# A bonus row spread earlier, and loads held behind a weight transfer, in a fused RWKV and feed-forward kernel

## The chip, the cores and the metric

One Trainium2 chip, one of its cores. The metric is the time of the whole program on the device in microseconds (us), taken several times for each kernel. "Span" is the length of the profiled execution, some 1.7 us less than its time.

## The reference, cut to what matters

A recurrent attention over 768 steps, for 4 batches and 8 heads of 48 columns, then a feed-forward layer over the 3072 rows that come out:

```python
for t in range(S):
    kt, vt, rt = k[:, :, t], v[:, :, t], r[:, :, t]
    cur = np.einsum('bhd,bhe->bhde', u[None] * kt, vt)          # the bonus, row u
    y[:, :, t] = np.einsum('bhd,bhde->bhe', rt, state + cur)
    state = w[None, :, :, None] * state + np.einsum('bhd,bhe->bhde', kt, vt)
x = y.transpose(0, 2, 1, 3).reshape(B * S, H * D)               # 3072 x 384
h = x @ w_in                                                    # 384 x 2048
out = (h * sigmoid(h)) @ w_out                                  # 2048 x 384
```

## The kernel before

The kernel works in 24 units: 6 pieces of 128 steps for each of 4 batches. A unit has three loads, r, k and v, each 128 steps x 8 heads x 48 columns: 1024 packets of 192 bytes. They go to six sets of tiles. In r and k each head's 48 columns stand in 64, so a row of 192 bytes starts every 256 bytes; in v the rows follow each other without gaps.

```python
rin = [big.tile([128, H, 64], FP, name=f"rin{i}") for i in range(NIN)]   # 6 sets
kin = [big.tile([128, H, 64], FP, name=f"kin{i}") for i in range(NIN)]
vin = [big.tile([128, H, D], FP, name=f"vin{i}") for i in range(NIN)]
# ... cut ...
load_row(nc.sync, wrow, w)
load(0, (0,), nc.scalar)        # r of unit 0 on ScalarE's queue
load_row(nc.scalar, urow, u)    # the bonus row behind it
load(0, (1,))
load(1, (0, 1))
load(0, (2,))
load(1, (2,))
for i in range(2, B):
    load(i)
```

At the start TensorE turns the row w into columns, transposes r of unit 0, turns the bonus row u into columns, transposes k of unit 0, and spreads u over 128 partitions (u_bc). GpSimd needs u_bc for its first product.

```python
spin(6)                         # matmuls on zeros, to keep TensorE going
wT = to_cols(wrow, None)
spin(3)
# ... cut ...
p1(0, mid=[cols_u, rows_u])     # between the transposes of r and of k
p1(1)
nat_ku(0)                       # GpSimd: k * u_bc
nat_rk(0)                       # GpSimd: r * that; VectorE then sums it per head
```

Later both halves of the second layer's weights (768 KB each) go on GpSimd's queue, and at about the same time the loads of units 6 to 9 on SyncE's:

```python
gate = cst.tile([128, 1], FP)
# ... cut ...
wout_part(0)
# ... cut ...
wout_part(1)
# ... cut ...
for i in range(4):
    load(NIN + i)               # units 6 to 9
p2(b_, nxt=b_ + 1, late=True)
```

## Time and profile before

| kernel before | us |
|---|---|
| median of 3 runs | 199.02 (198.54 to 199.46) |
| span of the profiled run | 197.3 |
| TensorE busy | 189.2 |
| first product of GpSimd starts | 8.19 |
| k of unit 8 lands | 51.3 |

TensorE is all but full. What can be won lies in a few waits of TensorE, and which ones they are is read in the prediction below. First, the queues' shares: packets, megabytes, and the time that the packets took as a share of all 16 DMA engines. The load queue q1 of the kernel before:

```profile
q1 hardware_dynamic: 84940, 20.46, 48.1%
```

Second, the work of ScalarE from 7.6 us on (start, length, engine, line, operation):

```profile
7.99 0.51 ACT L178 CAST v<-vin 128x384 f16<-128x384 f32 x1
8.41 1.28 ACT L441 ACTIVATE lamCT<-pif 112x128 f32<-112x128 f32 x4
...
11.79 1.91 ACT L214 ACTIVATE vu<-vin,rku 128x48 f32<-128x48 f32 x8 [1.70 <-DVE rku L200]
```

The eight bonus multiplications start at 11.79 us.

### The profile page before, as it was taken

To read this page: it belongs to the slowest core of one execution; us is meant where nothing else is said; L and a number is where in the kernel's file an instruction comes from. 1 tells how busy PE (TensorE), PEld (TensorE's weight loads), DVE (VectorE), ACT (ScalarE), POOL (GpSimd) and SP (SyncE) were. 2 spreads that over 40 slices of the span, in tenths; PEclk is the share of its full clock that TensorE was granted. 3 is DMA by queue.
4 is the path that set the end of the run, shared out by engine and by line. 5 is a ranking of instruction groups with operands and counts; after the bars stand their busy time and mean duration, and the time that the engine had idled before them with its cause. 6 is when DMAs were issued, how large, how long until landed. Compare 5 with 4: busy or idle time off the path is not lost.

```text
span 197.3 us, 4925 instructions
## 1 busy us (share of the span) xinstructions
PE 189.2 (96%) x1918; PEld 127.4 (65%) x1918; DVE 115.7 (59%) x233; ACT 91.0 (46%) x207; POOL 115.2 (58%) x145
## 2 busy tenths in 40 slices
PE   7969999899899999999999999999999999999993
PEld 2737878787666877675566766557666546644563
DVE  5867658885758764975675686476576344210121
ACT  3464587799311626215961216682016680069300
POOL 4389969989966859697669647735437710000000
PEclk9999999999999999999999999999999999999999
DMA  5999997999788754665567377526371011210022
GB/s 115 220 168 139 145 230 152 174 182 195 152 192 211 163 114 104 146 138 129 119 120 139 103 176 163 104 59 121 94 190 43 20 22 43 79 60 0 3 81 80
DMA packets 89696, 24.12 MB, mean 122 GB/s; under 512 B 82888, under 2 KB 89672, under 8 KB 89672
## 3 DMA queue, kind: packets, MB, share of 16 engines
q1 hardware_dynamic: 84940, 20.46, 48.1%
q0 software_dynamic: 3680, 3.15, 10.7%
q10 hardware_dynamic: 1052, 0.20, 0.5%
q8 instruction: 15, 0.25, 0.5%
q14 instruction: 9, 0.07, 0.1%
HBM read 20.45 MB, written 4.72 MB: 128 GB/s over the span
## 4 chain that ended last, share of the span: by engine, by line
PE 72%; POOL 11%; DMA 9%; issue 3%; SPq 1%; DVE 0%; POOLq 0%
PE ops L373 30%; PE hps L361 24%; DMA kin<-in_k_dram 9%; PE ae L270 8%; PE xs L245 4%; POOL ku L183 3%; POOL rku_f L189 3%; POOL kc L194 2%; PE y L296 2%; POOL win L416 2%; PE y L293 2%; POOL vu L206 1%; PE ops L387 1%; PE sps L312 1%; SPq L69 1%
## 5 line engine op out<-in xcount | busy, mean ns | idle before, releaser
L364 ACT ACTIVATE gT<-hps 128x256 f16<-128x256 f32 (+1 forms) x128 | 59.8, 494 | 50.5 <-PE hps L361 48.9
L361 PE MATMUL hps<-xT,win 128*128 128x256 f16 (+1 forms) x384 | 69.2, 326 | 0.2
L373 PE MATMUL ops<-wout,gT 128*128 128x384 f16 x368 | 63.8, 326 | 0.0
L361 PEld LDWEIGHTS <-win 128*128 128x128 f16 x384 | 35.4, 98 | 22.9 <-issue 0.7
L373 PEld LDWEIGHTS <-gT 128*128 128x128 f16 x368 | 34.7, 98 | 22.4
L279 DVE TENSOR_TENSOR am<-ae,maskM 128x512 f16<-128x512 f32 x24 | 16.6, 691 | 31.9 <-PE ao L272 31.8
L377 DVE COPY osb<-ops 128x384 f32<-128x384 f32 x23 | 12.7, 554 | 28.9 <-PE ops L373 28.7
L183 POOL TENSOR_TENSOR ku<-kin,u_bc 128x384 f32<-128x384 f32 x24 | 24.2, 1006 | 7.0 <-ACT u_bc L152 5.4
L270 PEld LDWEIGHTS ae<-rk 48*128 48x128 f32 x192 | 23.1, 187 | 7.3 <-issue 4.7
L206 POOL TENSOR_TENSOR vu<-vin,rku 128x384 f32<-128x384 f32 x23 | 19.1, 832 | 14.6 <-DVE rku L200 14.5
L272 PE MATMUL ao<-rk 48*128 48x128 f32 x192 | 27.5, 284 | 0.0
L270 PE MATMUL ae<-rk 48*128 48x128 f32 x192 | 27.5, 284 | 0.0
L256 DVE TENSOR_TENSOR rk<-xs,pif 112x512 f32<-112x512 f32 x40 | 25.6, 681 | 1.7 <-PE xs L245 1.7
L262 ACT CAST rT<-rk 112x512 f16<-112x512 f32 x20 | 12.3, 616 | 29.7 <-DVE rk L256 29.7
L189 POOL TENSOR_TENSOR rku_f<-rin,ku 128x384 f32<-128x384 f32 x24 | 24.1, 1004 | 1.9
L194 POOL TENSOR_TENSOR kc<-kin,lamC 128x384 f16<-128x384 f32 x24 | 24.0, 1004 | 0.0
L272 PEld LDWEIGHTS ao<-rk 48*128 48x128 f32 x192 | 23.1, 187 | 0.0
L303 DVE TENSOR_TENSOR y<-y,vu 128x384 f16<-128x384 f32 x24 | 13.4, 557 | 8.3 <-POOL kc L194 2.5
L326 POOL CAST stb<-st 112x384 f16<-112x384 f32 x12 | 6.1, 504 | 20.7 <-DVE st L321 20.7
L279 DVE TENSOR_TENSOR am<-ao,maskM 128x512 f16<-128x512 f32 x24 | 16.3, 680 | 0.0
L200 DVE TENSOR_REDUCE rku<-rku_f 128x8 f32<-128x384 f32 x24 | 13.2, 550 | 3.2 <-POOL rku_f L189 2.7
L296 PE MATMUL y<-v,am 128*128 128x48 f16 x192 | 12.2, 185 | 2.8 <-ACT st L452 1.5
(73 smaller groups left out, 170.5 us busy)
## 6 DMA issues: line engine op xcount, KB each, us to landing
kin<-in_k_dram SPq DMA_DIRECT2D x24, 192.0 KB, 3.4
vin<-in_v_dram SPq DMA_DIRECT2D x24, 192.0 KB, 3.7
rin<-in_r_dram SPq DMA_DIRECT2D x23, 192.0 KB, 3.4
out_dram<-osb SPq DMA_DIRECT2D x23, 192.0 KB, 1.9
win<-in_moe_w_in_dram POOLq DMA_DIRECT2D x4, 384.0 KB, 5.7
wout<-in_moe_w_out_dram POOLq DMA_DIRECT2D x2, 768.0 KB, 11.5
xT<-y SPq DMA_TRANSPOSE x18, 2.3
rin<-in_r_dram ACTq DMA_DIRECT2D x1, 192.0 KB, 2.7
```

The source lines that it names most:

```text
L183: nc.gpsimd.tensor_tensor(out=L["ku"], in0=kin[i % NIN][:, :, 0:D], in1=u_bc, op=ALU.mult)
L189: nc.gpsimd.tensor_tensor(out=L["rku_f"], in0=rin[i % NIN][:, :, 0:D], in1=L["ku"], op=ALU.mult)
L194: nc.gpsimd.tensor_tensor(out=kc[i % NKC][:, :, 0:D], in0=kin[n][:, :, 0:D], in1=lamC, op=ALU.mult)
L206: nc.gpsimd.tensor_tensor(out=L["vu"], in0=vin[i % NIN], in1=L["rku"].unsqueeze(2).broadcast_to([128, H, D]), op=ALU.mult)
L256: nc.vector.tensor_tensor(out=rk[:, :, :, 64 * g:64 * g + 64], in0=xs[g][0:PR], in1=lam(g), op=ALU.mult)
L270: nc.tensor.matmul(ae[:, p, :], L["kT"][0:D, p, :], L["rT"][0:D, p, :], start=True, stop=True)
L272: nc.tensor.matmul(ao[:, p, :], L["kT"][64:PR, p, :], L["rT"][64:PR, p, :], start=True, stop=True)
L279: nc.vector.tensor_tensor(out=am, in0=a, in1=maskM.unsqueeze(1).broadcast_to([128, NP, C]), op=ALU.mult)
L296: nc.tensor.matmul(y[:, 2 * p + j, :], L["am"][j][:, p, :], v16[:, 2 * p + j, :], start=not sc, stop=(not sc or j == 1))
L361: nc.tensor.matmul(hps, win[:, q, ft * 128:(ft + 1) * 128], xts[sc][:, q, b0:b1, :].rearrange("p b t -> p (b t)"), start=(q == 0), stop=(q ...
L364: nc.scalar.activation(out=gts[sc][:, ft, b0 * C:b1 * C], in_=hps, func=AF.Silu)
L373: nc.tensor.matmul(ops, gts[sc][:, ft, b * C:(b + 1) * C], wout[:, ft, :], start=(ft == 0), stop=(ft == NFT - 1))
```

## The change

It has two parts. The start: the bonus row goes alone onto ScalarE's queue, r of unit 0 joins SyncE's, and u is spread ahead of unit 0. The hold: a copy of 128 bytes out of the first half of the second layer's weights stands in SyncE's queue ahead of unit 8, so that the loads behind it wait until that half is in. The diff, cut to its core:

```diff
 load_row(nc.sync, wrow, w)
-load(0, (0,), nc.scalar)
 load_row(nc.scalar, urow, u)
-load(0, (1,))
+load(0, (0, 1))
 # ... cut ...
 spin(6)
 wT = to_cols(wrow, None)
-spin(3)
+spin(2)
+ucol = to_cols(urow, nc.scalar.copy)
+spin(2)
 u_bc = cst.tile([128, H, D], FP)
 # ... cut ...
+to_rows(u_bc, lambda p: ucol[:, p:p + 1].broadcast_to([PR, 128]))
 # ... cut ...
 gate = cst.tile([128, 1], FP)
+held = cst.tile([1, 64], F16)
 # ... cut ...
-p1(0, mid=[cols_u, rows_u])
+p1(0)
 # ... cut ...
-for i in range(4):
-    load(NIN + i)
+load(NIN)
+load(NIN + 1)
+nc.sync.dma_start(out=held, in_=wout[0:1, 0, 0:64])
+load(NIN + 2)
+load(NIN + 3)
```

More of the change, by code (lines that the diff above doesn't have):

```diff
@@ L62, in unit, with load @@
         return divmod(i, B)
-    def load(i, which=(0, 1, 2), queue=nc.sync):
+    def load(i, which=(0, 1, 2)):
         if i >= NU:
@@ L68, in load @@
         for t, src in [((rin, r), (kin, k), (vin, v))[x] for x in which]:
-            queue.dma_start(out=t[i % NIN][:, :, 0:D],
+            nc.sync.dma_start(out=t[i % NIN][:, :, 0:D],
                               in_=src[b, :, sc * C:sc * C + C, :]
@@ L215, in bonus_act, with p1 @@
                                  func=AF.Copy, scale=L["rku"][:, h:h + 1])
-    def p1(i, spins=0, mid=()):
+    def p1(i, spins=0):
         n = i % NIN
@@ L226, in p1 @@
                 nc.tensor.transpose(t[0:PR, p, :], flat[:, 128 * p:128 * p + PR], ident)
-            if mid:
-                mid.pop(0)()
         rk = wrk.tile([PR, 2, NP, C], FP, name="rk")
@@ L422, in wout_part @@
             in_=moe_w_out[1024 * g:1024 * g + 1024, :].rearrange("(f p) n -> p f n", p=128))
-    def cols_u():
-        live["u"] = to_cols(urow, nc.scalar.copy)
-    def rows_u():
-        to_rows(u_bc, lambda p: live["u"][:, p:p + 1].broadcast_to([PR, 128]))
-    p1(0, mid=[cols_u, rows_u])
+    p1(0)
     p1(1)
```

## The prediction

> **What bounds the kernel now.** I read the page first (engine shares and the chain that ended last), then TensorE's waits, then the order of time on GpSimd, VectorE and TensorE in the first 20 us, and last the queue of SyncE with the DMA queues between 34 and 53 us.
>
> ```profile
> span 197.3 us, 4925 instructions
> PE 189.2 (96%) x1918; PEld 127.4 (65%) x1918; DVE 115.7 (59%) x233; ACT 91.0 (46%) x207; POOL 115.2 (58%) x145
> ```
>
> TensorE is busy for 189.2 of 197.3 us. 1.26 us pass before its first matmul and about 3 us after its last, so only some 4 us of idle time lie inside the program, and no change that leaves the arithmetic alone can win more than that. The waits of TensorE name it:
>
> ```profile
> PE y L296 <- ACT st L452: 1.5, 1, 1.5
> PE y L296 <- DVE am L279: 1.3, 4, 0.4
> PE spin L128 <- DVE wrow L80: 1.3, 1, 1.3
> PE xs L245 <- DMA kin<-in_k_dram: 0.5, 1, 0.5
> ```
>
> Two single waits matter, the first (at 13 to 14.5 us) and the last (at 50.7 to 51.3 us). After the second I find no further wait of TensorE up to its last matmul: from 51.7 us on whatever time TensorE has gained stays gained.
>
> The first wait is labelled with a ScalarE copy (L452) that ends at 14.48 us. I do not believe the label: the first weight load of that group waits on VectorE's semaphore, and the VectorE mask ends at 14.45 us. Its own history is this (start, length, engine, line, operation):
>
> ```profile
> 13.30 0.55 DVE L200 TENSOR_REDUCE rku<-rku_f 128x8 f32<-128x384 f32 x1 [1.54 <-POOL rku_f L189]
> 13.77 0.68 DVE L279 TENSOR_TENSOR am<-ae,maskM 128x512 f16<-128x512 f32 x1
> ```
> ```profile
> 8.19 1.01 POOL L183 TENSOR_TENSOR ku<-kin,u_bc 128x384 f32<-128x384 f32 x1 [5.45 <-ACT u_bc L152]
> 9.28 1.00 POOL L189 TENSOR_TENSOR rku_f<-rin,ku 128x384 f32<-128x384 f32 x1
> 10.22 0.93 POOL L416 DMA_DIRECT2D win<-in_moe_w_in_dram  x1
> 11.17 1.01 POOL L183 TENSOR_TENSOR ku<-kin,u_bc 128x384 f32<-128x384 f32 x1
> 12.27 1.00 POOL L189 TENSOR_TENSOR rku_f<-rin,ku 128x384 f32<-128x384 f32 x1
> ```
>
> GpSimd sits idle 5.45 us for u_bc, the bonus row spread over 128 partitions, then works without a break; VectorE's second reduction waits 1.54 us for GpSimd's second product; the mask of unit 1 stands behind that reduction, and TensorE behind the mask. So the arrival of u_bc at 8.1 us decides the first wait. The chain that ended last says the same: up to 34 us it runs on GpSimd.
>
> The second wait is for k of unit 8. SyncE's queue around it:
>
> ```profile
> 35.20 0.71 SPq L69 DMA_DIRECT2D rin<-in_r_dram  x1
> 36.02 0.71 SPq L69 DMA_DIRECT2D kin<-in_k_dram  x1
> 36.81 5.45 SPq L69 DMA_DIRECT2D vin<-in_v_dram  x1
> 42.36 4.85 SPq L69 DMA_DIRECT2D rin<-in_r_dram  x1
> 47.32 3.54 SPq L69 DMA_DIRECT2D kin<-in_k_dram  x1
> ```
>
> The k load is issued at 36.02 us and lands at 51.3 us, against a median of 3.4 us from issue to landing. In those 15 us both halves of the second layer's weights (issued by GpSimd at 34.96 and 38.45 us) are on the same engines. Counting packets by microsecond: from 43 to 48 us the weight queue moves about 190 packets of 768 bytes per us and the load queue about 190 of 192 bytes; alone the load queue moves some 1200. SyncE also stands still[...]. The first half of the weights lands at 45.5 us, the second at 50.8 us; their first use is at 48.0 us.
>
> **What the Trainium skill says.** "DMA: Bandwidth & Descriptors", section "Queues, rings and completion order": each DMA engine takes turns between the rings that have work, a packet at a time. The trace agrees with its 190 against 190 packets per us: a small packet pays one large packet's turn, which is why the loads crawl at about 36 KB per us. The same page, section "Issuing engines are not separate DMA queues": starting transfers from several engines saves only sequencer time. Here that is half true: r of unit 0 on ScalarE's queue began moving at about 1.9 us, while the SyncE queue had nothing to move before 2.9 us. "TensorE: Matmul & The Clock Gate", section "What's actually happening": the array runs at half rate until it has been busy for a window of about 3.4 us. The trace: 427 ns per 512-column matmul until about 6 us, 216 ns afterwards. So operations put ahead of unit 0 cost double.
>
> **The change part by part.**
>
> (1) The bonus row moves to the head of ScalarE's queue. It was issued at 1.28 us and landed at 3.6; the row w, issued at 0.81 us, landed at 3.4. I take 3.2 to 3.4 us. That alone is little: it was not the landing that held u_bc but its place on TensorE behind the transposes of r of unit 0 (6.36 us for the columns, 7.03 us for the rows).
>
> (2) The two steps move ahead of unit 0. The columns of w end at 4.12 us; two spins take 399 + 426 ns to 4.95; the columns of u start at about 5.08; two spins (start 5.27) run to 6.10 and cover ScalarE's small copy (about 5.4 to 5.5 us). Rows: four 112-column transposes, 97 ns each warm, some 190 cold; with the clock rising near 6.4 us two and two make 0.57, end 6.67. ScalarE started its copy 0.20 us after the last row's slot (7.42 to 7.62), so now at 6.87; 0.49 us gives 7.36, GpSimd starts at about 7.44. Against 8.19 that is 0.75 us earlier. The second product then ends at about 12.5, the reduction at 13.1, the even mask at 13.7, and TensorE goes on at 13.76 instead of 14.51. One spin more (4 for 3) lies inside this.
>
> Unit 0's own transposes start at 6.67 instead of 5.37. VectorE could not use them before 7.03, when it had its powers of w; the first set is now there at about 7.2. The four groups of transposes end at about 8.4 (8.3 before). Cost about 0.1 to 0.2 us on TensorE and VectorE, all ahead of the wait that GpSimd sets: nothing on the path.
>
> (3) r of unit 0 goes to SyncE's queue: one load of 196 KB more there, at about 235 KB per us, 0.83 us. All later first loads land that much later: k of unit 1 at about 7.6 us (6.77 before), needed by TensorE at 7.9; v of unit 0 at about 8.6, needed in the second product at 10.8. A near tie for the first, room for the rest. The first part of the first layer's weights landed at 17.0 with its use at 17.5; its start moves with GpSimd, so I keep that margin.
>
> (4) From 14 to 50 us TensorE, GpSimd and the loads that GpSimd gates move together. The 0.75 us should survive to 50 us, unless a transfer does not move with them.
>
> (5) The small copy out of the first half of the weights sits in SyncE's queue ahead of unit 8. The first half then has the engines to itself as soon as unit 7 is in. A pair of packets takes 16/190 us = 84 ns of an engine, a load packet alone 13 ns (16/1200), so a weight packet 71 ns: 1024 packets alone take 4.5 us against 5.4. Starting at about 36.4 instead of 37.2 us, it is in at about 41 us on most engines and, with the lag of 1.3 us that the last two engines showed, lands at 42.3. Unit 8 is then issued at about 42.9. About 350 packets of the second half remain when the loads start to flow (44.0); these share until 45.9, then the loads run at 1200 per us: r of unit 8 lands at about 46.5, k at 47.3, with a slow engine at 48.5 to 49. TensorE wants k at 51.30 - 0.55 - 0.75 = about 50.0. The wait of 0.55 us should go. The copy itself is 128 bytes.
>
> Sum: 0.75 + 0.55 = 1.3 us. I take off 0.1 for what moves unevenly: 199.0 - 1.2 = 197.8 us.
>
> **The rivals.** (a) Holding the loads makes them later still: between 21 and 24.8 us, with the first layer's weights flowing, the load queue moved nothing although r of unit 4 had been issued at 20.37. If the loads of unit 8 get no turn before the second half is through (about 45.5 us), k lands at about 47.4, on slow engines 49: still in time. With a second lag of 2 us, as at 51.3 before, a wait of up to 1 us stays: 198.3 to 198.8. (b) The start gives nothing, because the wait passes to another: k of unit 1 late by some tenths, or the ScalarE copy labelled in the list (it has to come after eight bonus multiplications of 1.9 us and does not move). Then only 0.55 is left: 198.5. Against it speaks VectorE's 1.54 us of waiting for GpSimd. (c) The gain of the start is swallowed between 20 and 50 us, by the loads of units 4 and 5: k of unit 5 landed at 31.86 and was used at 31.91, two of its sixteen engines 2 us behind. If that does not move, 0.3 to 0.7 us goes: about 198.3. (d) More than the sum: shorter waits of 0.2 to 0.4 us at 26, 38.7 and 39.9 us also shrink: 197.1.
>
> **Range and chances.** The sum gives 197.8; (a), (b) and (c) each pull up by 0.5 to 1, (d) down by 0.7; the three runs of before already spread over 0.9. I say 197.0 to 198.7. Faster by over 2% needs 195.0, that is 4 us, as much as all the idle time inside: 1%. Slower by over 2% needs a new wait of over 5 us that nothing suggests: 1%.
>
> **What would show it.** Right: GpSimd's first product at about 7.4 us; the wait before unit 1's y at about 0.8 instead of 1.5; the first half of the weights landing near 42 us; k of unit 8 landing before 49 us with no wait of TensorE for it; everything after 52 us earlier by the same 1.2 to 1.3 us. Wrong: u_bc still at 8 us or a new wait for k of unit 1 near 8 us; an unmoved second wait, or one for v, x or the output copies behind SyncE's held queue; a shift at 20 us that has vanished by 45.

## The result, and the profile after

The changed kernel took 198.60 us (median of 6 runs, 198.40 to 198.93), the kernel before in the same rounds 199.09 (198.54 to 199.46). The ratio is 0.9979, with a 95% interval of 0.9961 to 0.9996. Ratios here and below compare the fast runs of the same rounds, and lie near the ratio of the means without being quite equal to it. The means are 198.64 and 199.07: 0.43 us were won where 1.2 had been forecast.

The page of the kernel after begins:

```profile
span 197.2 us, 4928 instructions
PE 189.9 (96%) x1919; PEld 127.6 (65%) x1919; DVE 115.5 (59%) x233; ACT 91.1 (46%) x207; POOL 115.1 (58%) x145
```

The profiled execution (198.93 us) is the slowest of the six, so its span has hardly moved. TensorE's waits in it (engine, line waited for: us in all, times, longest):

```profile
PE y L297 <- DVE am L280: 1.4, 4, 0.4
PE spin L127 <- DVE urow L80: 1.3, 1, 1.3
PE tk L229 <- DMA kin<-in_k_dram: 0.5, 1, 0.5
PE yT L350 <- DVE y L304: 0.5, 2, 0.3
PE hps L362 <- DMA win<-in_moe_w_in_dram: 0.2, 1, 0.2
```

Both waits of the prediction have shrunk: no single one before y is over 0.4 us now, and the one for k of unit 8 no longer makes the list. But new ones have come, for k of unit 1 (L229) and for the first layer's weights (L362). In the order of time, GpSimd, TensorE and ScalarE of the kernel after:

```profile
7.57 1.01 POOL L186 TENSOR_TENSOR ku<-kin,u_bc 128x384 f32<-128x384 f32 x1 [4.84 <-ACT u_bc L153]
```
```profile
8.82 0.62 PE L229 MATMUL tk<-ident,kin 128*112 128x128 f32 x4 [0.54 <-DMA kin<-in_k_dram]
```
```profile
9.77 0.51 ACT L181 CAST v<-vin 128x384 f16<-128x384 f32 x1 [2.29 <-DMA vin<-in_v_dram]
10.19 1.27 ACT L437 ACTIVATE lamCT<-pif 112x128 f32<-112x128 f32 x4
...
12.78 1.91 ACT L217 ACTIVATE vu<-vin,rku 128x48 f32<-128x48 f32 x8 [0.91 <-DVE rku L203]
```

GpSimd's first product comes 0.62 us earlier (7.57 for 8.19), as planned. ScalarE now stands 2.29 us for v of unit 0, and its bonus multiplications start at 12.78 instead of 11.79, a whole us later. What they waited for last is VectorE's sum (L203). It stands behind the masks of unit 0 (10.99 us instead of 10.01), and these stand behind the late transposes of k of unit 1 on TensorE. The late result then holds up VectorE by 0.29 us, and TensorE behind it by as much (yT, L350, at 15.34 us):

```profile
10.99 0.69 DVE L280 TENSOR_TENSOR am<-ae,maskM 128x512 f16<-128x512 f32 x1 [0.83 <-PE ao L273]
14.72 1.02 DVE L304 TENSOR_TENSOR y<-y,vu 128x384 f16<-128x384 f32 x2 [0.29 <-ACT vu L217]
```
So the loads have come to set the pace, where u_bc did.

The same moments of TensorE in both traces, with two experiments to come (us from the span's start; "k of 6" is the start of the transposes of k of unit 6):

| | y of unit 1 | first first-layer matmul | r of unit 4 | k of 6 | k of 8 | last matmul |
|---|---|---|---|---|---|---|
| before | 14.51 | 17.52 | 27.67 | 36.19 | 51.30 | 194.09 |
| after | 13.89 | 17.28 | 27.58 | 36.41 | 51.28 | 194.08 |
| e13, after again | 13.84 | 17.27 | 28.18 | 36.82 | 51.49 | 194.25 |
| e14, after with a larger tile | 13.81 | 16.82 | 26.98 | 35.50 | 49.90 | 192.65 |

The kernel after is 0.62 us ahead at 13.9 us, 0.24 at 17.3, 0.09 at 27.6 and behind at 36.4. The gain is all but gone at 27.6 us, before the hold begins (SyncE stands from 35.7 us on). What differs between the two in those 30 us is the load queue. Its lines on the page of the kernel after (packets, megabytes, share of 16 engines), and the start of the table of stages, 3 to 13 us (TensorE, weight loads, VectorE, ScalarE, GpSimd, clock, DMA share, GB/s), first of before, then of after:

```profile
q1 hardware_dynamic: 86012, 20.65, 60.8%
q0 software_dynamic: 3680, 3.15, 10.6%
```
```profile
3.00:13.00 10.00, 9.64 (x78) 6.27 (x76) 6.66 (x16) 4.85 (x16) 4.64 (x5) 1.00 1.08 203
```
```profile
3.00:13.00 10.00, 9.11 (x76) 6.05 (x75) 7.02 (x17) 3.50 (x11) 4.90 (x5) 1.00 1.38 175
```

The queue carries all 72 loads now, one more than before (r of unit 0), yet its packets take 60.8% in place of 48.1%: 0.608 x 16 x 197.2 / 86012 is 22.3 ns for a packet, where it was 17.9. And from 3 to 13 us the packets took more of the engines' time (1.38 for 1.08; a sum over packets that overlap, so it can pass 1) and moved less (175 GB/s for 203). The queue of weights, q0, is as it was. Counting the DMA records of the trace alone, the 192-byte packets of the loads take 15 ns when all goes well; 3.9% of them take more than 20 ns before, 33.0% after, and this from 4 us on, over 30 us before the hold begins.

The hold did this to SyncE's queue of the kernel after (held is the copy of 128 bytes; next to it the loads of r and k of unit 8):

```profile
44.23 0.64 SPq L548 DMA_DIRECT2D held<-wout  x1
44.96 0.53 SPq L69 DMA_DIRECT2D rin<-in_r_dram  x1
45.60 0.52 SPq L69 DMA_DIRECT2D kin<-in_k_dram  x1
```

The first half of the weights landed at 44.2 us (45.5 before), the second at 48.2 (50.8 before), and k of unit 8 at 51.24 (51.3 before).

### The profile page after: what moved, and what is told of

Its sections match the earlier page's. It is cut to its first block, busy times and chain, and to the rows that moved or that the text cites. A ratio compares the mean times of both kernels' runs of the same rounds, so it can differ in the third digit from the quotient of the medians.

```text
span 197.2 us, 4928 instructions
## 1 busy us (share of the span) xinstructions
PE 189.9 (96%) x1919; PEld 127.6 (65%) x1919; DVE 115.5 (59%) x233; ACT 91.1 (46%) x207; POOL 115.1 (58%) x145
## 3 DMA queue, kind: packets, MB, share of 16 engines
q1 hardware_dynamic: 86012, 20.65, 60.8%
## 4 chain that ended last, share of the span: by engine, by line
PE 83%; DMA 6%; DVE 3%; POOL 3%; SPq 2%; issue 1%; ACT 0%; DVEq 0%; POOLq 0%
PE ops L374 31%; PE hps L362 29%; PE ae L271 11%; DMA kin<-in_k_dram 6%; PE xs L246 4%; PE y L297 2%; PE y L294 2%; DVE am L280 2%; PE sps L313 2%; PE ops L388 1%; SPq L69 1%; POOL win L418 1%; PE ao L273 1%; POOL ku L186 1%; POOL rku_f L192 1%
## 5 line engine op out<-in xcount | busy, mean ns | idle before, releaser
L362 PE MATMUL hps<-xT,win 128*128 128x256 f16 (+1 forms) x384 | 69.2, 326 | 0.4 <-DMA win<-in_moe_w_in_dram 0.2
L362 PEld LDWEIGHTS <-win 128*128 128x128 f16 x384 | 35.3, 98 | 23.3 <-issue 0.8
L186 POOL TENSOR_TENSOR ku<-kin,u_bc 128x384 f32<-128x384 f32 x24 | 24.2, 1007 | 7.8 <-ACT u_bc L153 4.8
L203 DVE TENSOR_REDUCE rku<-rku_f 128x8 f32<-128x384 f32 x24 | 13.1, 550 | 2.1 <-POOL rku_f L192 1.5
L181 ACT CAST v<-vin 128x384 f16<-128x384 f32 x24 | 12.2, 506 | 4.2 <-DMA vin<-in_v_dram 4.2
```

What stands on the lines that cost most here:

```text
L186: nc.gpsimd.tensor_tensor(out=L["ku"], in0=kin[i % NIN][:, :, 0:D], in1=u_bc, op=ALU.mult)
L362: nc.tensor.matmul(hps, win[:, q, ft * 128:(ft + 1) * 128], xts[sc][:, q, b0:b1, :].rearrange("p b t -> p (b t)"), start=(q == 0), stop=(q ...
```

## The experiments

Sixteen kernels, in four calls; those of a call ran on one chip in the same rounds as the kernel before. Each entry gives the median, the range, and the ratio with its 95% interval. No ratio here is as far as 2% from 1: all is about tenths of a per cent.

**First call: the parts apart** (before in these rounds: 198.39, 197.15 to 199.62, 11 runs). The kernel before spreads over 2.5 us here, more than all that is in dispute; keep it in mind for every ratio.

*e1: the start alone.*

```diff
 # from the kernel after
-held = cst.tile([1, 64], F16)
-nc.sync.dma_start(out=held, in_=wout[0:1, 0, 0:64])
```

> The changed kernel without the held copy: row u alone on the ScalarE queue and spread ahead of unit 0, r of unit 0 on the SyncE queue, loads of units 8 and 9 not held. Theory A (the end is pinned by the landing of k of unit 8 near 51.2 us, and the hold does not move that landing because the loads get no turn until the weights are through): same as the changed kernel, ratio to before 0.996 to 0.999. Rival B (the hold earns the 0.4 us, the start nothing): ratio 0.999 to 1.001. Rival C (the start earns it and the hold costs some): ratio 0.992 to 0.996.

197.50 us (196.87 to 197.95), ratio 0.9964 (0.9923 to 1.0005). The mean is 0.84 us below before's. Its first product started at 6.72 us, and TensorE met no wait for k of unit 8, though the loads were not held: that k landed at 46.0 us.

*e2: the hold alone*, on the old start.

```diff
 # from the kernel before
+held = cst.tile([1, 64], F16)
-for i in range(4):
-    load(NIN + i)
+load(NIN)
+load(NIN + 1)
+nc.sync.dma_start(out=held, in_=wout[0:1, 0, 0:64])
+load(NIN + 2)
+load(NIN + 3)
```

> The kernel before with only the held copy ahead of unit 8. Theory A: k of unit 8 lands within 0.5 us of where it landed before (51.3 us), TensorE still waits 0.3 to 0.8 us for it, ratio 0.998 to 1.001, though the first half of the weights lands 1 us or more earlier. Rival B: k of unit 8 lands before 50 us, no wait, ratio 0.996 to 0.998. Rival C: ratio 1.001 to 1.005.

198.99 us (198.74 to 199.39), ratio 1.0043 (1.0004 to 1.0082): slower by some 0.4%, just clear of its interval. TensorE waited 0.5 us at 24.2 and 0.6 us at 26.6 us for the first layer's weights, before any load is held. So something in this edit harms the part of the program that lies ahead of the hold, and its waiting cannot be what does it.

*e3: r of unit 0 back on ScalarE's queue, behind u.*

```diff
 # from the kernel after
-load(0, (0, 1))
+load(0, (0,), nc.scalar)
+load(0, (1,))
```

> The changed kernel with r of unit 0 put back on the ScalarE queue, but behind row u. If moving r of unit 0 to SyncE ate the gain of the start (k of unit 1 at 8.7 instead of 6.8 us, v of unit 0 at 9.7 instead of 7.8, eight bonus multiplications 1 us later): k of unit 1 lands near 7.2 us, no wait of TensorE for it, unit 1's y goes on at about 13.8 us and the shift at 17.5 us is 0.6 to 0.8 us instead of 0.24; ratio to before 0.993 to 0.997 if the shift survives, 0.997 to 0.999 if the landing of k of unit 8 pins the end anyhow (theory A).

198.69 us (198.11 to 199.08), ratio 1.0020 (0.9976 to 1.0064): no gain over e4. r of unit 0 did land early, at 6.4 us, but k of unit 1 still at 8.8. One load less ahead of it on SyncE's queue did not bring it forward, so the extra load on that queue is not what makes it late here.

*e4: the kernel after once more*, unchanged.

> The changed kernel once more, on the same chip. In its profile a third of the 192-byte load packets took over 20 ns, against 4 per cent in the profile of before. If that belongs to the run and not to the change, this profile or its times differ: spans from 196.7 to 197.2 us, as the six runs on record show, and a profile with few slow packets lies at the lower end. If it belongs to the change, a third of the packets is slow here too. Ratio 0.996 to 0.999.

198.45 us (198.29 to 198.80), ratio 1.0016 (0.9977 to 1.0055). Here there is no gain at all. Taken together, e1 is better than e4 by 1.0 us on the same chip: the line that holds the loads, or its tile, takes away all that the start brings.

Of the four, e2, e3 and e4 had slow packets like the kernel after (29.1%, 31.7%, 32.8% over 20 ns), and e1 had not (4.0%). What the three share is the 128-byte tile held. The built program's table of addresses shows what it does: it lies ahead of the load tiles, so all of them move by 128 bytes. Without it the first tile of r starts 32 bytes after a multiple of 256, with it 160 bytes after. A row of r or k (192 bytes, every 256) then runs over a multiple of 256, from 160 to 352; before, it lay inside, from 32 to 224. The Trainium skill, "DMA: Bandwidth & Descriptors", section "How a descriptor splits into AXI transactions", says that a transaction starts at a 256-byte boundary even where the descriptor does not; by its way of counting the moved row needs two transactions and the old one needs one. It says so of what is read and gives no time for a destination in SBUF, so this was a theory to test: the place of the tiles, not the hold, takes the gain. The rival was that the held copy or the loads' new place in time slows the queue.

**Second call: the place of the tiles** (before: 198.31, 197.08 to 199.47).

*e5: the kernel after, with a tile of 256 bytes*, of which the copy uses the same 128. The tiles are back at 32.

```diff
-held = cst.tile([1, 64], F16)
+held = cst.tile([1, 128], F16)
-nc.sync.dma_start(out=held, in_=wout[0:1, 0, 0:64])
+nc.sync.dma_start(out=held[:, 0:64], in_=wout[0:1, 0, 0:64])
```

> The changed kernel with one number altered: the tile that the held copy fills has 128 elements (256 bytes) instead of 64 (128 bytes); the copy is the same 128 bytes. In all kernels with the 128-byte tile, every tile allocated after it lies 128 bytes higher, so that the 192-byte rows of r and k start at 160 of a 256-byte block and run over its end, instead of at 32 and inside it; with 256 bytes they are inside again. Layout theory: slow load packets (over 20 ns) fall from about 30 to about 4 per cent, k of unit 1 lands near 7.5 instead of 8.7 us, the span falls from 196.6 to 197.2 to about 195 to 195.8, ratio to the kernel before 0.988 to 0.996. Rival (the held copy itself, or the chip's mood, slows the loads): share of slow packets stays near 30 per cent, ratio 0.997 to 1.002.

197.58 us (197.30 to 198.19), ratio 0.9981 (0.9929 to 1.0033). Slow packets 1.2%. With the same hold the slow packets are gone. The time is too loose by itself.

*e6: the kernel before, with the tile and one small fill of it*; no copy, no hold, the old start.

```diff
 gate = cst.tile([128, 1], FP)
+held = cst.tile([1, 64], F16)
+nc.gpsimd.memset(held, 0.0)
```

> The kernel before with an unused tile of 128 bytes at the same place, and one tiny fill of it while GpSimd is idle; no held copy. Layout theory: about 30 per cent slow load packets, loads about 1.05 us each instead of 0.87, ratio to before 1.002 to 1.010. Rival: 4 per cent slow, ratio 0.999 to 1.001.

198.41 us (198.06 to 200.41), ratio 1.0030 (0.9975 to 1.0084). The load queue's line of e6:

```profile
q1 hardware_dynamic: 84940, 20.46, 60.0%
```

Packet for packet and byte for byte the queue of before (84940, 20.46 MB), and yet 60.0% for 48.1%; 34.1% of the loads' packets over 20 ns. A tile of 128 bytes that nothing reads does it. This strikes out the rival as the cause of the slow packets. And TensorE meets two waits, as it does in e2, that neither profile of before has:

```profile
PE hps L361 <- DMA win<-in_moe_w_in_dram: 0.7, 1, 0.7
PE tk L226 <- DMA kin<-in_k_dram: 0.4, 1, 0.4
```

The price in time is not to be read from this run: one of its six took 200.41 us, and the interval is wide.

*e7: the hold alone, with 256 bytes* (e2 with the tile of e5).

> The kernel before with the held copy alone, into a 256-byte tile: the hold without the shift of the layout and without the new start. If the hold is good by itself: k of unit 8 lands before 49.5 us, no wait of TensorE for it, ratio 0.995 to 0.998. If it does nothing, since the loads get no turn until the second half of the weights is through: 0.999 to 1.002, with k of unit 8 landing at 49 to 51.5 us.

198.22 us (197.13 to 199.14), ratio 1.0007 (0.9956 to 1.0059). The harm of e2 does not show here (another chip, and the two intervals overlap), and the hold by itself brings nothing that can be measured. Its profiled run was the fastest, 197.13 us, and shows that the old start itself varies: GpSimd's first product is at 7.14 us,

```profile
7.14 1.00 POOL L183 TENSOR_TENSOR ku<-kin,u_bc 128x384 f32<-128x384 f32 x1 [4.41 <-ACT u_bc L152]
```

against 8.19 in the profile of before. Nothing in the program differs up to there but 256 bytes of layout that leave the offsets alone. What differs is when TensorE goes over from 427 to 216 ns for a 512-column matmul: between 3.4 and 4.6 us here, between 6.0 and 6.8 in the profile of before. Ahead of u_bc stand transposes that cost double until then.

*e8: e3 without the hold and its tile*: the new start, r of unit 0 on ScalarE's queue behind u.

> The new start without the hold (no new tile, layout as before), with r of unit 0 on the ScalarE queue behind row u. If sharing the SyncE queue costs the start anything with fast loads: k of unit 1 lands near 7.0 instead of 7.5 us, ratio against the run with r of unit 0 on SyncE (197.5 us) lower by 0.1 to 0.3 us; if not, the same within 0.2 us: ratio to before 0.992 to 0.998.

196.96 us (196.82 to 197.65), ratio 0.9946 (0.9899 to 0.9992). Faster than the kernel before, just clear of the interval. k of unit 1 landed at 6.97 us (7.51 in e1, 8.69 after), so there is no wait for it. The edit that brought k of unit 1 no further forward in e3 does so once the tiles lie well. That it is worth time beyond e1 is not shown (0.9946 and 0.9964 on two chips, with intervals that overlap).

**Third call: the rest** (before: 198.37, 197.18 to 199.05).

*e9: the kernel before, one look*, for a second profile of it.

> The kernel before, unchanged, for one more profile. Clock theory: its runs spread from 197.1 to 199.6 us because TensorE's change to the full rate falls anywhere from 4.5 to 6.5 us into the run; in this kernel the row u is spread behind four transposes of unit 0, so GpSimd's first product moves with it. Expected: change of rate near 4.5 us goes with a first product at about 7.1 us and a time of 197 to 197.5 us; near 6.3 us with 8.2 us and 199 to 199.5 us. Rival (something later, such as the landing of k of unit 8, makes the spread): times that do not follow the first product.

198.42 us, one run, state unknown. The first product at 8.35 us, the change of clock between 6.8 and 7.1, and no wait for k of unit 8 at all, in its place one of 0.4 us for k of unit 5:

```profile
PE xs L245 <- DMA kin<-in_k_dram: 0.4, 1, 0.4
```

So the 0.55 us of k of unit 8 that the prediction counted on belongs to one execution, not to the kernel.

*e10: e8 again.*

> The best kernel so far once more (new start, no hold, r of unit 0 on the ScalarE queue behind row u), for comparison on one chip with the next two: 196.8 to 197.6 us, ratio 0.990 to 0.997.

197.64 us (196.75 to 197.96), ratio 0.9965 (0.9931 to 0.9999). The gain holds on another chip; by the numbers it is somewhat smaller, but the intervals overlap.

*e11: e8 with the hold and 256 bytes.*

> The same with the held copy into a 256-byte tile: the hold without the shift of the layout. If the hold is worth the 0.55 us of my prediction also here: 196.4 us. If k of unit 8 lands in time without it (45.6 us without the hold, wanted at about 48.5), the hold can only delay: 196.9 to 197.6 us, k of unit 8 landing at 46 to 48 us, the weights landing 2 us or more earlier with nobody waiting for them.

197.25 us (196.77 to 197.65), ratio 0.9946 (0.9911 to 0.9982). 0.28 us below e10 in the mean, with intervals that overlap: the hold does no harm here and cannot be shown to help.

*e12: e8 with the bonus sum of unit 1 later*, so that its reduction on VectorE does not stand ahead of the mask.

```diff
 p2(0, spins=2)
 bonus_sum(0)
-bonus_sum(1)
 nat_v(1)
 bonus_act(0)
-bonus_vu(1)
 p2(1)
+bonus_sum(1)
+bonus_vu(1)
 p3y(0)
```

> The same without the hold, and with the reduction of unit 1 on VectorE put behind its two masks (the values are the same). The profile of this start still shows TensorE waiting 0.78 us ahead of unit 1's y for masks that stand behind that reduction. If that wait is on the path: it falls below 0.3 us and the time by 0.3 to 0.6 us, 196.4 to 196.7 us. If GpSimd, which then gets the sums of unit 1 about 0.4 to 0.9 us later, is the bound: same or up to 0.5 us slower.

197.68 us (197.16 to 198.49), ratio 0.9976 (0.9941 to 1.0011): nothing won over e10. TensorE's wait before y of unit 1 did go, and two others came:

```profile
PE yT L351 <- POOL vu L210: 0.8, 1, 0.8
PE ops L375 <- DMA wout<-in_moe_w_out_dram: 0.6, 1, 0.6
```

A wait that moves is not a wait that goes: the reduction still has to be made, and what needs it now comes later.

**Fourth call: the place alone, on one chip** (before: 199.07, 197.40 to 199.29). Four times the changed kernel, only the size of the tile differs.

*e13: the kernel after once more* (128 bytes, offset 160).

> The changed kernel (tile of 128 bytes; rows of r and k start at 160 of a 256-byte block and cross its end), as partner of the next three on one chip: load queue share near 60 per cent, 198.3 to 198.8 us.

198.87 us (198.68 to 199.18), ratio 1.0003 (0.9972 to 1.0035).

*e14: 256 bytes* (offset 32), e5 again.

> The changed kernel with a tile of 256 bytes (rows start at 32 and end at 224, no crossing): load queue share near 48 per cent, 197.3 to 198.2 us, 0.5 to 1.2 us faster than its partner on the same chip. If the loss does not come from the layout: the same as its partner within 0.2 us.

197.48 us (197.08 to 197.90), ratio 0.9934 (0.9904 to 0.9963).

*e15: 32 bytes* (offset 64).

```diff
-held = cst.tile([1, 64], F16)
+held = cst.tile([1, 16], F16)
-nc.sync.dma_start(out=held, in_=wout[0:1, 0, 0:64])
+nc.sync.dma_start(out=held, in_=wout[0:1, 0, 0:16])
```

> The changed kernel with a tile and a copy of 32 bytes: everything after it lies 32 bytes higher, rows of r and k start at 64 and end exactly at 256. Crossing theory: no row of r or k crosses, share near 48 per cent, 197.3 to 198.2 us. Rival, any shift from 32 costs (or any held copy into a tile shorter than 256 bytes): share near 60 per cent, 198.3 to 198.8 us.

197.68 us (197.02 to 198.62), ratio 0.9947 (0.9914 to 0.9980).

*e16: 64 bytes* (offset 96), which the copy fills.

```diff
-held = cst.tile([1, 64], F16)
+held = cst.tile([1, 32], F16)
-nc.sync.dma_start(out=held, in_=wout[0:1, 0, 0:64])
+nc.sync.dma_start(out=held, in_=wout[0:1, 0, 0:32])
```

> The changed kernel with a tile and a copy of 64 bytes: rows of r and k start at 96 and end at 288, crossing by 32 bytes. Crossing theory: as slow as with 128 bytes, share 55 to 61 per cent, 198.2 to 198.8 us. Rival, only a shift by 128 costs: share near 48 per cent, 197.3 to 198.2 us.

198.75 us (198.46 to 199.27), ratio 1.0001 (0.9971 to 1.0031).

The load queue's line of e13, e14, e15 and e16 in turn:

```profile
q1 hardware_dynamic: 86012, 20.65, 59.9%
```
```profile
q1 hardware_dynamic: 86012, 20.65, 49.1%
```
```profile
q1 hardware_dynamic: 86012, 20.65, 48.3%
```
```profile
q1 hardware_dynamic: 86012, 20.65, 60.5%
```

The same packets and bytes, two levels and nothing between. All layouts side by side ("over" says whether a row of r or k runs over a multiple of 256; the slow packets are counted from the DMA records):

| kernel | tile | a row of r or k from, to | over | q1's share | loads' packets over 20 ns |
|---|---|---|---|---|---|
| before | none | 32, 224 | no | 48.1% | 3.9% |
| e8 | none | 32, 224 | no | 49.2% | 4.0% |
| e14 | 256 bytes | 32, 224 | no | 49.1% | 1.3% |
| e15 | 32 bytes | 64, 256 | no | 48.3% | 1.1% |
| e16 | 64 bytes | 96, 288 | yes | 60.5% | 31.1% |
| after | 128 bytes | 160, 352 | yes | 60.8% | 33.0% |
| e6 | 128 bytes, unused | 160, 352 | yes | 60.0% | 34.1% |

From e13 to e14 the mean falls from 198.90 to 197.48: 1.42 us on one chip, for a tile that is larger and not smaller, and the slowest run of e14 (197.90) is faster than the fastest of e13 (198.68). From e16 to e15 it falls by 1.08; there one run of e15 (198.62) lies among those of e16. The tile moves more than the loads' tiles: the weights, the states and others lie behind it too. But the engines' own operations take no longer for it (mean of GpSimd's first product 1008 ns in e13 and 1006 in e14, of VectorE's mask 692 in both, of TensorE's second-layer matmul 326 in both), so the loads are what is left. What TensorE waited for in e14, and SyncE's held copy with the loads behind it:

```profile
PE y L297 <- DVE am L280: 1.9, 5, 0.6
PE spin L127 <- DVE urow L80: 1.3, 1, 1.3
PE yT L350 <- DVE y L304: 0.2, 1, 0.2
```
```profile
41.73 0.63 SPq L548 DMA_DIRECT2D held<-wout  x1
42.45 0.54 SPq L69 DMA_DIRECT2D rin<-in_r_dram  x1
43.10 0.52 SPq L69 DMA_DIRECT2D kin<-in_k_dram  x1
```

No DMA is left in the list of waits, and the first half of the weights is in at 41.7 us where the kernel after had it at 44.2. k of unit 8 landed at 47.1 us and was wanted at 49.9. In the table of moments above, e14 keeps its 0.7 us from 13.8 to 36 us and has 1.4 at the end.

What stays open is why. "A row that runs over a multiple of 256 is slow" is too simple. In v, whose rows follow each other, three rows of four run over in both kinds of layout (two of four at offset 64), and there the v loads are fast where r and k do not run over. In the kernel after, the first load of a burst is fast even though it runs over (of units 12 to 23, with the packets given to the loads in order of time, r has 0 to 3% slow packets in all units but one, k 12 to 31% in all but one, v 25 to 69%). What in a burst makes the later loads slow, no run measured by itself.

## Why the prediction was wrong

The forecast was 1.2 us, with 1.3 as the sum; measured were 0.43 us, and in the repeats e4 and e13 none. The step that failed is that of the loads: (3) and (4) took their rate from the kernel before, and (5) added a tile that slows them, from 17.9 to 22.3 ns for a packet. That cost 1.4 us (e13 to e14), more than the whole forecast. The 0.55 us of step (5) failed too, for another reason: the wait did not belong to the kernel. By its steps:

- Steps (1) and (2), the bonus row earlier: right. The first product was forecast at 7.44 us and came at 7.57, y of unit 1 at 13.76 and 13.89. The transposes of the rows took 0.71 us up to the next operation, not 0.57, as the clock changed only at 6.7 to 6.9 us. The 0.75 us also hold where it changes at another time: with a change between 4.5 and 5.5 us the first product is at 7.62 and 7.63 us in the old start (e2, e6) and at 6.56 to 6.88 in the new one (five profiles), with one after 6 us at 8.19 and 8.35 (before, e9) and at 7.37 to 7.64 (six profiles).
- Step (3) failed. "One load of 196 KB more there ... 0.83 us" and "k of unit 1 at about 7.6 us" took the load rate of the kernel before as given. k of unit 1 came at 8.69 us, v of unit 0 at 9.75 instead of 8.6. In e14, the same program with the tiles at their old offsets, k of unit 1 landed at 7.9 and TensorE did not wait for it. So 0.8 of the 1.1 us that k of unit 1 missed its forecast by is the layout. The rest of the near tie is real: in e5, the same program on another chip, k came at 8.0 and TensorE still waited 0.4 us for it.
- Step (4), "the 0.75 us should survive to 50 us", failed for the same reason: 0.24 us were left at 17.3 us and nothing at 36. In e14 0.69 were left at 36 us. Plainest is e13: its first product came at 6.88 us and y of unit 1 still only at 13.84; in e1, without the tile, a first product at 6.72 us led to y at 13.06. The prediction's rival (c), loads that swallow the gain, is what happened, but from 9 us on and not only between 20 and 50, and not for units 4 and 5 alone.
- Step (5) says "The copy itself is 128 bytes" and counts only its transfer. It never asked where the 128 bytes lie. That is the missing term: e13 and e14 measure it at 1.4 us, e16 and e15 at 1.1; pairs of different calls (e2 and e7, e4 and e5) give about 0.7 each by their ratios. It is about as large as the whole forecast gain.
- Step (5) also took 0.55 us for the wait for k of unit 8. It was a chance of that one profile. TensorE had no such wait in e9, the kernel before again, nor in e1 and e8, which hold nothing. The hold's own worth is not measurable (e7 against before 1.0007; e11 against e10 0.28 us, overlapping). Its steps were right in kind: the first half of the weights was forecast to land at 42.3 us and landed at 41.7 in e14. One reading in it is too wide: 190 packets against 190 holds from 44 to 48 us, while from 42 to 44 the load queue moved 310 to 330 a us.
- Rival (a), held loads that get no turn, was seen in part: the first packets of r of unit 8 moved 2.0 us after the start of their issue in e14, against 1.2 us for r of unit 0 in the same run. In the kernel after, it was 1.2 us for both. In e14 the held k of unit 8 cost nothing (47.1 us, used at 49.9); in the kernel after it landed at 51.24, just ahead of its use at 51.28.

Whether the change with the tile repaired is worth what was forecast is not settled. Against all runs of before in the same rounds e14 is 1.34 us better and e15 1.08, but e5, the same program as e14 on another chip, only 0.48. The loose end is the kernel before, which ran from 197.1 to 199.6 us, where e14 ran from 197.1 to 197.9. Two things about it:

- The clock's change at the start moves its first product by 1.2 us (7.14 in e7 to 8.35 in e9). But it moves that of the new start as much, and e9, with the latest, took less than the profiled run of before.
- Each run in the four calls has a mean granted clock of TensorE beside it. Of the 44 runs of before, 15 show 0.989 to 0.991 and took 199.0 to 199.6 us; the other 29 show 0.998 or more and took 197.1 to 199.05. Against these 29 alone, call by call, the gain is 0.70 us in e14, 0.44 in e15, 0.28 in e1 and none in e5. With the new start, none of 78 runs shows a clock under 0.998; with the old one, e2 has one such run of six and e7 two. So a good part of what the start is worth may be that these runs do not occur with it.

No such run was profiled (every trace shows 0.998 or more), so why they occur stays open. The best versions are those with r of unit 0 on ScalarE's queue behind u and the tiles at offset 32: 196.96 (e8), 197.64 (e10), 197.25 (e11).

## What to carry to other kernels

Before you count what a small added tile does, ask where it lies and what stands behind it: look at the addresses of the load tiles in the built program and at their queue's share, before and after. Pad it so that the rows keep their offset, and an experiment that undoes a change has to keep the layout too, or it compares two things. Look at the granted clock of each run before you compare means. And take a wait into a forecast only when a second profile of the same kernel shows it again.

## What the Trainium skill lacked or had wrong

- No page tells that the offset of a load's rows in SBUF sets its speed. One unused tile of 128 bytes took the load queue from 48.1% to 60.0% of the engines (e6), and a larger one gave 1.42 us back (e13 to e14). It would belong to "DMA: Bandwidth & Descriptors", section "How a descriptor splits into AXI transactions". That section speaks of what is read; here the source stayed and the destination moved. Its count of transactions agrees in direction for r and k. Its count of beats (32 bytes each) does not: worked out by its rule it is 7, 8, 9 and 11 for a row at offset 32, 64, 96 and 160, and 96 is as slow as 160 (60.5% and 60.8%). And by either count v (three rows of four over a boundary) should be slow in the good layouts too, and there 1.1 to 4.0% of all load packets were.
- "TensorE: Matmul & The Clock Gate", section "What you observe", gives the change of clock at around 4 us of activity, within 500 ns from run to run. Here the first matmul starts at 1.26 us and the change fell between 3.4 to 4.6 us (e7) and 6.8 to 7.1 us (e9) of the span, so between about 2 and 6 us of activity over these chips and runs, and it moved the first product of one and the same start from 7.14 to 8.35 us.
